# Writing the product kv into the space of ssm_k with an 8-byte step between the columns that TensorE loads

## The chip, the cores and the metric

One core of a Trainium2 chip. The metric is the device time of one execution in microseconds (us); lower is better. Kernels are compared only within the same rounds.

## The reference, cut to what matters

```python
# A: q, k, v are (1, 2048, 512), ssm_k is (512, 2048), shift_k is (512, 4)
kv = shift(k, shift_k) * v                       # 4 taps along the sequence, then a product
kv_f = rfft(pad(kv));  kf_f = rfft(pad(ssm_k))   # along the sequence, length 4096
y    = irfft(kv_f * kf_f)[:2048] + kv * ssm_D
h    = x + layernorm(x) * y                      # x is q
out  = h + relu(layernorm(h) @ w1) @ w2          # 512 -> 1376 -> 512
```

The kernel does the Fourier transforms as two stages of matmuls, with position t = 64 n1 + n2. Both inputs of the transform, ssm_k and kv, lie with the 512 features on partitions (four row groups of 128). Before stage 1 TensorE turns them, so that (row group, n1) comes to lie on partitions: 64 transposes each, one per n2.

## The kernel before: the parts that matter

```python
sk = early.tile([P, DC, S], BF16, name="sk")                 # ssm_k, one DMA
nc.sync.dma_start(out=sk[:], in_=A_ssm_k.rearrange("(c p) t -> p c t", p=P))
vT = vp.tile([P, DC, S], BF16, name="vT")                    # v, one tile filled by four DMAs
for c in range(4):
    ts = slice(CH * c, CH * c + CH)                          # CH = 512
    nc.sync.dma_start_transpose(out=kT[:, :, 16 + CH * c:16 + CH * c + CH], in_=k_d[ts, :])
    nc.sync.dma_start_transpose(out=vT[:, :, ts], in_=v_d[ts, :])
# ... [cut]
def to_rows(src, q, fl, eng):
    pst = psum.tile([P, 8, P], BF16, tag="ps", name="pst")
    for i in range(8):                                       # columns 64 elements = 128 bytes apart
        nc.tensor.transpose(out=pst[:, i, :], in_=src[:, :, :, 8 * q + i], identity=ident[:])
    copy(eng, fl[:, :, :, 8 * q:8 * q + 8], pst[:].rearrange("p i (d g) -> p g d i", d=2))
# ... [cut]
skv = sk[:].rearrange("p c (a b) -> p c a b", b=64)
for q in range(8):
    to_rows(skv, q, kfl, "DADADADA"[q])                      # D: VectorE, A: ScalarE

def taps(u):                                                 # 16 units: chunk c of 512, row group rg
    c, rg = divmod(u, DC)
    ps = psum.tile([P, CH], F32, tag="ps", name="pkv")
    for j in range(KS):
        nc.tensor.matmul(out=ps[:], lhsT=wdiag[:, rg, j, :], rhs=kT[...], start=..., stop=...)
    vv = vT[:, rg, CH * c:CH * c + CH]
    nc.vector.tensor_tensor(out=vv, in0=ps[:], in1=vv, op=ALU.mult)    # kv, in place

taps(0)
for gb in range(7):
    group_k(gb)                                              # stage 1 of ssm_k, and a table
    taps(2 * gb + 1)
    taps(2 * gb + 2)
taps(15)
group_k(7)
# ... [cut]
kvv = vT[:].rearrange("p r (a b) -> p r a b", b=64)
for q in range(8):
    to_rows(kvv, q, xfl, "ADADADAD"[q])                      # again 128 bytes apart
# then: spectrum of k and stage 1 of kv; products (psy); first inverse stage (psi);
# second inverse stage (pz); the two matmuls of the MLP (ps1m, ps2m)
```

`rearrange` only describes another view of the same bytes. The framework derives all waits from the views of the tiles, and decides which of a tile's writers an instruction waits for.

## Time and profile before

| | before |
|---|---|
| time, median of 3 | 223.93 us (223.79 to 223.94) |
| profiled span, mean granted clock | 221.4 us, 0.999 |
| first k transposition, first stage-1 group of k | 9.73, 17.16 |
| first kv transposition, first stage-1 group of kv | 37.48, 45.44 |
| first psi, pz, ps1m matmul | 98.44, 114.97, 128.09 |

The last three rows are times from the start of the span, read off the chain of waits. The profile lines themselves stand in the prediction.

### The profile page before, as it was taken

The numbers are of one execution on the slowest core, as the hardware profiler recorded it, in microseconds if no ns is written. First come the engines' busy times: TensorE is split into PE (matmuls) and PEld (weight loads), VectorE is DVE, ScalarE is ACT, GpSimd is POOL, SyncE is SP. The second block draws the span as 40 slices with busy tenths as digits, with TensorE's granted clock in tenths as the row PEclk, the third lists the DMA queues.
The fourth block names the chain that finished last, engine by engine and source line by source line (L and its number), as shares of the span: only waits on it lengthen the run. The fifth ranks groups of instructions, "written<-read, shape, count | busy, mean of one in ns | idle before, by whom it ended". The sixth has DMA issues, their size and how long they took to land.

```text
span 221.4 us, 7288 instructions
## 1 busy us (share of the span) xinstructions
PE 201.6 (91%) x3111; PEld 140.1 (63%) x3111; DVE 150.3 (68%) x299; ACT 133.0 (60%) x252; POOL 72.0 (33%) x103
## 2 busy tenths in 40 slices
PE   0299799999989999989989899999999999999993
PEld 0294446999978999969977578544444444444452
DVE  4898788889997999966878779761973257130031
ACT  2868877888885888867983889103650066206500
POOL 8399940000008999978400120220022002000000
PEclk9999999999999999999999999999999999999999
DMA  5999920000000000019990000152113110421012
GB/s 178 311 223 204 193 53 4 0 4 6 3 3 3 1 0 0 4 47 238 258 340 14 3 3 3 24 82 58 31 28 80 42 48 4 95 56 42 0 43 54
DMA packets 30384, 15.41 MB, mean 70 GB/s; under 512 B 25520, under 2 KB 29072, under 8 KB 30224
## 3 DMA queue, kind: packets, MB, share of 16 engines
q1 hardware_dynamic: 29520, 14.76, 29.0%
q8 instruction: 24, 0.39, 0.7%
q10 hardware_dynamic: 832, 0.20, 0.4%
q14 instruction: 8, 0.07, 0.1%
HBM read 7.08 MB, written 2.10 MB: 41 GB/s over the span
## 4 chain that ended last, share of the span: by engine, by line
PE 85%; ACT 5%; DMA 4%; DVE 2%; issue 1%; SPq 0%; DVEq 0%; ACTq 0%
PE ps2m L536 18%; PE ps1m L524 16%; PE pz L450 8%; PE psy L343 7%; PE psi L417 7%; PE pkv L262 6%; PE pst L203 6%; PE ps L221 4%; PE ps2k L236 4%; DMA sk<-in_A_ssm_k_dram 4%; PE ps2k L238 3%; PE u L236 3%; PE u L238 3%; ACT ecore L131 1%; ACT zt L461 1%
## 5 line engine op out<-in xcount | busy, mean ns | idle before, releaser
L526 ACT ACTIVATE h1T<-ps1m 128x512 bf16<-128x512 f32 (+3 forms) x55 | 27.4, 514 | 21.2 <-PE ps1m L524 20.3
L524 PE MATMUL ps1m<-hlnT,w 128*128 128x512 bf16 (+3 forms) x220 | 39.6, 336 | 0.3
L536 PE MATMUL ps2m<-w,h1T 128*128 128x512 bf16 (+3 forms) x187 | 39.8, 367 | 0.0
L538 DVE TENSOR_TENSOR o<-ps2m,xh 128x512 bf16<-128x512 f32 (+1 forms) x17 | 11.1, 659 | 37.6 <-PE ps2m L536 32.2
L524 PEld LDWEIGHTS <-w 128*128 128x128 bf16 (+1 forms) x220 | 21.7, 100 | 17.6 <-issue 1.4
L536 PEld LDWEIGHTS <-h1T 128*128 128x128 bf16 (+1 forms) x187 | 17.6, 98 | 21.2 <-issue 3.1
L333 DVE TENSOR_TENSOR t<-u,kf 128x704 fp32r<-128x704 f32 x32 | 26.7, 883 | 3.0 <-ACT usb L329 2.8
L333 POOL TENSOR_TENSOR t<-usb,kf 128x320 fp32r<-128x320 f32 x32 | 28.2, 935 | 1.4 <-ACT usb L329 1.0
L461 ACT CAST zt<-pz 128x512 bf16<-128x512 f32 x16 | 8.4, 593 | 29.5 <-PE pz L450 29.5
L450 PE MATMUL pz<-bp,ecore 32*32 32x128 f32 x1024 | 23.1, 384 | 1.7 <-DVE bp L210 0.9
L470 POOL TENSOR_SCALAR rstd<-mv 128x4 f32<-128x4 f32 (+1 forms) x7 | 1.6, 232 | 70.1 <-DVE mv L477 70.1
L208 ACT CAST a<-ps 128x512 fp32r<-128x512 f32 (+1 forms) x38 | 19.3, 568 | 4.3 <-PE ps L221 4.3
L450 PEld LDWEIGHTS pz<-bp,ecore 32*32 32x32 f32 x1024 | 14.4, 103 | 9.1 <-issue 5.0
L210 DVE CAST a<-ps 128x512 fp32r<-128x512 f32 (+1 forms) x30 | 18.5, 651 | 2.2 <-PE ps L221 2.1
L208 ACT CAST kf<-psy 128x512 fp32r<-128x512 f32 x30 | 17.4, 641 | 1.8 <-PE psy L343 0.3
L475 DVE BATCH_NORM_STATS2 st<-xh 128x6 f32<-128x512 bf16 x28 | 17.3, 678 | 0.0
L262 PE MATMUL pkv<-kT,wdiag 128*128 128x512 bf16 x64 | 15.4, 380 | 1.2 <-issue 1.2
L417 PE MATMUL psi<-dre,kf 128*128 128x256 f32 x64 | 15.5, 284 | 0.9 <-DVE kf L210 0.9
L343 PE MATMUL psy<-t,ipos 128*128 128x512 f32 x48 | 15.9, 391 | 0.0
L417 PE MATMUL psi<-dim,kf 128*128 128x256 f32 x64 | 15.4, 283 | 0.0
L203 PE MATMUL pst<-ident,sk 128*128 128x128 bf16 x64 | 6.3, 277 | 9.7 <-DMA sk<-in_A_ssm_k_dram 9.7
L265 DVE TENSOR_TENSOR vT<-pkv,vT 128x512 bf16<-128x512 f32 x16 | 10.9, 691 | 3.4 <-PE pkv L262 3.4
(113 smaller groups left out, 394.9 us busy)
## 6 DMA issues: line engine op xcount, KB each, us to landing
sk<-in_A_ssm_k_dram SPq DMA_DIRECT2D x1, 2048.0 KB, 8.4
out_dram<-o SPq DMA_DIRECT2D x58, 32.0 KB, 1.6
xh<-in_A_q_dram SPq DMA_DIRECT2D x4, 384.0 KB, 6.8
w<-in_B_w_dram SPq DMA_DIRECT2D x1, 1376.0 KB, 12.8
w<-in_B_w_dram SPq DMA_DIRECT2D x1, 1280.0 KB, 16.2
xh<-in_A_q_dram SPq DMA_DIRECT2D x4, 128.0 KB, 2.8
hlnT<-hln SPq DMA_TRANSPOSE x12, 2.4
w<-in_B_w_dram SPq DMA_DIRECT2D x1, 96.0 KB, 15.9
```

Of the source, the lines that this page charges most:

```text
L203: nc.tensor.transpose(out=pst[:, i, :], in_=src[:, :, :, 8 * q + i], identity=ident[:])
L208: nc.scalar.copy(out=o, in_=i)
L210: nc.vector.tensor_copy(out=o, in_=i)
L262: nc.tensor.matmul(out=ps[:], lhsT=wdiag[:, rg, j, :], rhs=kT[:, rg, CH * c + 16 - j:CH * c + CH + 16 - j], start=(j == 0), stop=(j == KS ...
L333: eng.tensor_tensor(out=t[:, :, j, :], in0=in0.unsqueeze(1).to_broadcast([P, 2, n, 2]), in1=kfr[:, :, j, ks], op=ALU.mult)
L343: nc.tensor.matmul(out=psy[:], lhsT=m_[:], rhs=t_.rearrange("p j k -> p (j k)"), start=first, stop=not first)
L417: nc.tensor.matmul(out=ps[:, i, :], lhsT=kf[:, c, 4 * m:4 * m + 4, :].rearrange("p r k -> p (r k)"), rhs=d[:].rearrange("p a b -> p (a b)" ...
L450: nc.tensor.matmul(out=pz[32 * a:32 * a + 32, r4, l4, :], lhsT=ecore[rows, rho, n2, :], rhs=rhs, start=(rho == 0), stop=(rho == 1), tile_p ...
L475: nc.vector.bn_stats(out=st[:, t % 4, :], in_=xh[:, t, :])
L524: nc.tensor.matmul(out=ps1[:fsz, :], lhsT=w1[:, c, fc * P:fc * P + fsz], rhs=hlnTs[sc][:, c, part], start=(c == 0), stop=(c == DC - 1))
L526: nc.scalar.activation(out=h1s[sc][:fsz, fc, part], in_=ps1[:fsz, :], func=ACT.Relu)
L536: nc.tensor.matmul(out=ps2[:], lhsT=h1s[sc][:ksz, fc, i * P:(i + 1) * P], rhs=w2[:ksz, fc, ds], start=(fc == 0), stop=(fc == NFC - 1))
```

## The change

Its intent: a weight load whose columns lie 128 bytes apart is slow (204 ns against 97), so kv is written in another order, (n2 // 4, row group, n1, n2 % 4), where the columns of one load lie 8 bytes apart. That order cannot be written in place, so kv goes into the space of ssm_k. Four smaller parts come with it: ssm_k in two halves with column-tiled transposes, one more taps unit ahead of the first group, other shares of the copies, and split copies at two ends.

```diff
-    nc.sync.dma_start(out=sk[:], in_=A_ssm_k.rearrange("(c p) t -> p c t", p=P))
+    for h in range(2):
+        nc.sync.dma_start(out=sk[:, 2 * h:2 * h + 2, :], in_=A_ssm_k[2 * h * P:(2 * h + 2) * P, :]...)
 ...
-    for q in range(8):
-        to_rows(skv, q, kfl, "DADADADA"[q])
+    psts = [psum.tile([P, 8, P], BF16, tag="ps", name="pst") for _ in range(8)]
+    for h in range(2):
+        hs = slice(64 * h, 64 * h + 64)
+        for q in range(8):
+            for i in range(8):
+                nc.tensor.transpose(out=psts[q][hs, i, :], in_=skv[:, 2 * h:2 * h + 2, :, 8 * q + i],
+                                    identity=ident[:], tile_position=(0, 64 * h))
+            if h == 1:
+                rows_out(psts[q], q, kfl, "DADADADA"[q])
 ...
+    kvx = sk[:].rearrange("p c t -> p (c t)").rearrange("p (h r a l) -> p h r a l", h=16, r=DC, l=4)
 ...
-        vv = vT[:, rg, CH * c:CH * c + CH]
-        nc.vector.tensor_tensor(out=vv, in0=ps[:], in1=vv, op=ALU.mult)
+        split = "p (a h l) -> p a h l"
+        nc.vector.tensor_tensor(out=kvx[:, :, rg, 8 * c:8 * c + 8, :].rearrange("p h a l -> p a h l"),
+                                in0=ps[:].rearrange(split, h=16, l=4),
+                                in1=vT[:, rg, CH * c:CH * c + CH].rearrange(split, h=16, l=4), op=ALU.mult)
 ...
     taps(0)
-    for gb in range(7):
+    taps(1)
+    for gb in range(8):
         group_k(gb)
-        taps(2 * gb + 1)
-        taps(2 * gb + 2)
-    taps(15)
-    group_k(7)
+        for u in range(2 * gb + 2, min(2 * gb + 4, 16)):
+            taps(u)
 ...
-        to_rows(kvv, q, xfl, "ADADADAD"[q])
+        pst = psum.tile([P, 8, P], BF16, tag="ps", name="pst")
+        for i in range(8):
+            nc.tensor.transpose(out=pst[:, i, :],
+                                in_=kvx[:, 2 * q + i // 4, :, :, i % 4].rearrange("p r a -> p (r a)"), identity=ident[:])
+        rows_out(pst, q, xfl, "ADADADAD"[q])
 ...  [cut: other shares of the stage-1 copies; the last two psy copies and two psi copies split over both engines]
```

## The prediction

> **What bounds the kernel now.** I read the page first (TensorE busy 91% of 221.4 us, the next, VectorE, 68%; TensorE is 85% of the chain that ended last), then that chain over the stages that the diff touches:
>
> ```profile
> 1.25 8.44 DMA sk<-in_A_ssm_k_dram
> 9.69 0.05 issue
> 9.73 6.34 PE pst L203 x64
> 16.07 0.02 issue
> 16.09 1.02 ACT kfl L208
> 17.11 0.04 issue
> 17.16 0.68 PE ps L221 x64
> 17.84 1.83 PE pkv L262 x8
> ...
> 25.77 1.24 issue
> 27.02 1.46 PE pkv L262 x6
> ...
> 36.73 0.70 DVE vT L265
> 37.43 0.04 issue
> 37.48 5.99 PE pst L203 x64
> ```
>
> Columns are start, length, what. TensorE waits for the whole of ssm_k until 9.73, transposes it (L203), then alternates one stage-1 group (0.61) with two taps units (8 matmuls, 1.83) at 2.45 us a group, then transposes kv (37.48 to 43.47), then does spectrum and stage 1 at 2.72 us a group, TensorE back to back. So anything that shortens TensorE's work or starts it earlier before about 45 us moves the end by as much, unless a copy takes over.
>
> How fast are the transposes? Their weight loads step 128 bytes between columns (64 bf16). Counted in equal stretches (TensorE busy with its count, then its weight loads):
>
> ```profile
> 9.73:12.73 3.00, 3.00 (x28) 3.00 (x29) 1.00 1.13 247
> 12.83:15.83 3.00, 3.00 (x38) 3.00 (x35) 1.00 1.19 229
> 37.48:40.48 3.00, 3.00 (x33) 3.00 (x34) 1.00 0.02 5
> ```
>
> The first 3 us hold 28 starts, one per 107 ns; the other 36 k transposes start in the 3.1 us after that, one per 86 ns (the second row also counts those still in flight at its start), and those of kv one per 91 to 94 ns (5.99 / 64). Transposes late in the kernel read contiguous columns:
>
> ```profile
> 125.85 0.61 PE L546 MATMUL pz<-ident,hln 128*128 128x128 bf16 x8 [0.43 <-ACT zt L461]
> ```
>
> Eight in 0.61, of which the last one's own duration is 0.22: (0.61 - 0.22) / 7 = 56 ns each. A contiguous load is recorded at 97 ns, the strided one of kv at 204. So the kv transposes are bound by the strided load, 36 ns above what the moving operand needs.
>
> Their copies out of PSUM (busy us, mean ns):
>
> ```profile
> L210 DVE COPY xfl<-pst 128x1024 bf16<-128x1024 bf16 x4 | 4.9, 1225 | 1.2 <-PE pst L203 0.6 <-issue 0.6
> L208 ACT COPY xfl<-pst 128x1024 bf16<-128x1024 bf16 x4 | 3.9, 1012 | 0.5 <-PE pst L203 0.4
> ```
>
> **What the Trainium skill says.** (1) "SBUF — State Buffer", "Door 1: The DMA port swizzle", its note on cachelines: 16-byte lines, at least two hits on a line are needed for full bandwidth. At 128 bytes a line gives one hit, at 8 bytes two. The trace agrees for the two ends (94 against 56 ns) and shows nothing at 8 bytes. (2) "TensorE: Matmul & The Clock Gate", Part 1: start to start is N / 1.2 GHz while the clock is gated (106.7 ns for N = 128), N / 2.4 GHz plus 2.5 ns after about one busy window of 3.4 us, the window free-running. The trace agrees: 107 ns for 3.07 us, and 56 where loads are contiguous. The clock column above says 1.00 throughout and doesn't show the gate. (3) "TensorEngine Tiling (Array Packing)", "Restrictions": column tiling disables the fast weight load. The changed k transposes are column tiled; no row of this trace shows such a load with a stride. (4) "Advanced Engine Details and Errata", "ISA Cache": instructions are cached in lines of 16 KB, 256 instructions. The profile has 24 packets of 0.39 MB on the instruction queue, 16 KB each. I read the 1.24 us "issue" at 25.77 as a late fetch: no data is awaited there, and the DMA share of that time is full of transposes.
>
> **The change part by part.**
>
> (a) ssm_k in two halves; 128 transposes of 64 columns in place of 64 of 128. Half of the big packets had ended by 5.95, all by 9.23, and TensorE started 0.5 later, so the first half releases it at about 6.45 instead of 9.73: 3.3 us earlier. But each transposition still streams 128 columns of the identity, so the number of full-length streams doubles, and the first ones run gated. With the gate opening 3.1 us after the start (as before), 29 are done by 9.6 and 99 x 0.056 = 5.5 end at 15.1; with the gate opening only at 12.8, 59 are done and 69 x 0.056 = 3.9 end at 16.7. Middle 15.9, against 16.09 before. So this part nearly pays for itself and no more, up to here.
>
> (b) Two taps units, not one, stand before the first stage-1 group. Before, TensorE had done one when it waited for the last kfl copy until 17.16. Now both follow the transposes: 15.9 + 2 x 0.92 = 17.75, by when the copies are done (VectorE 4 x 1.2 from about 12.5, ScalarE less). The first group starts at 17.75, 0.6 later, with 0.92 more behind it: 0.3 gained. The last group now stands after the last taps as before, so the 0.7 of VectorE at 36.73 stays.
>
> (c) Instruction fetch. The stall came 705 TensorE instructions (loads and matmuls) in; the extra 128 bring that point one group (144) earlier, to about 25, when its fetch is asked for before the third k transfer fills the queues. I take a third of the 1.24 as remaining: 0.8 gained, anywhere from 0 to 1.24.
>
> Sum so far: kv transposes start 1.1 us earlier, near 36.4 (range 0 to 2.3).
>
> (d) kv written with an 8-byte stride. TensorE: 64 x (94 - 56) = 2.4 us less. But copies then bind. From the start T of the transposes, VectorE still has two stage-1 copies until T + 1.2 (37.36 + 1.29 in the trace), then four of 1.225: T + 6.1. ScalarE has two copies and two table pieces until T + 2.0 (39.37), then four of 1.01: T + 6.05. The first kv stage-1 group needs all eight. Before it started at 45.37 = T + 7.9; now at T + 6.2. Gained: 1.7, not 2.4. The product itself writes runs of four bf16 instead of rows; its 691 ns are set by 512 fp32 read from PSUM, and the spectrum addition that writes pairs of fp32 takes 682, so I give it no cost.
>
> (e) In spectrum and stage 1, three copies of 0.69 move from VectorE to ScalarE (0.54 each). VectorE falls from 2.57 to an average near 2.3 per 2.72 group, ScalarE rises from 2.4 to 2.95 in odd groups, 2.66 on average. TensorE stays the bound; it prevents the backlog from (d) from growing, and may cost 0.1.
>
> (f) End of products: the last two copies are split, but the instruction order shows that the VectorE half waits for the ScalarE half of the same PSUM tile. ScalarE 0.35 then VectorE 0.41 is no faster than one VectorE copy of 0.69: 0. End of the first inverse stage:
>
> ```profile
> 113.11 1.35 ACT L208 COPY bp<-psi 128x512 f32<-128x512 f32 x3 [0.37 <-PE psi L417]
> ...
> 113.48 0.68 DVE L405 BATCH_NORM_STATS2 st<-xh 128x6 f32<-128x512 bf16 x1
> ...
> 114.19 0.18 DVE L406 BATCH_NORM_AGGREGATE mv<-st 128x2 f32<-128x6 f32 x1
> 114.47 1.28 ACT L467 ACT_TABLE_LOAD   x1
> 114.49 0.42 DVE L210 COPY bp<-psi 128x256 f32<-128x256 f32 x1
> ```
>
> VectorE is busy with statistics until 114.37 and now has two half copies instead of one: 114.37 + 2 x 0.4 = 115.15 against 114.91. Lost: 0.25.
>
> Sum: 1.1 + 1.7 - 0.1 - 0.25 = 2.45 us. After 68 us nothing else changes. 223.93 - 2.45 = 221.5.
>
> **The rivals.**
>
> Rival A, any stride loses the fast load: contiguity, not the line, decides. For it: a contiguous fp32 load, which is four bytes per column, is recorded at 188 ns, like the strided bf16. Against: the two-hits rule. Then the kv transposes stay at 94 ns, (d) gives 0, and the time is 223.2.
>
> Rival B, the column-tiled strided load is slow. [...]if a far column costs 88 / 32 = 2.75 ns on its own, 64 take 176 ns, the 128 end near 29 instead of 15.9, and the kernel takes about 234. Against: during the gated 3 us, 128 such columns loaded within 107 ns. If it is 70 to 80 ns instead of 56, (a) loses 1.4 to 2.4 on the last 99 and the time is near 223.
>
> Rival C, everything goes well: gate open at 9.6, no fetch stall. The first group starts at 17.0, kv transposes at 35.1: 2.3 gained, sum 3.7, time 220.2. More than 2% needs 219.5, that is 4.4 us, which these parts reach only if phase (e) speeds up too; TensorE back to back there speaks against it.
>
> Rival D, the start is late (gate at 12.8) and the fetch stall stays whole: (a) to (c) give -0.5 and the time is 223.1.
>
> **Range and chances.** Centre 221.5. The middle of A and D gives the upper end 223.3, C with a little from PSUM waits avoided gives 219.9. More than 2% faster: 0.07. Slower by over 2% (above 228.5) needs B in full: 0.03. Within 2%: 0.90.
>
> **What would show it.** The first transposition near 6.4 and the last near 15.9; first stage-1 group of k at 17.75; the count of kv transposes in 3 us near 53 rather than 33; kfl and xfl copies unchanged in length; the first kv stage-1 group 6.2 us after the first kv transposition, released by a copy and no longer by TensorE; 2.7 us a group after it; the "issue" gap shorter or gone; the first pz matmul 0.25 later relative to the last psi matmul. I am wrong on (a) if column-tiled transposes start more than 65 ns apart after the gate opens, on (d) if the kv ones stay above 80 ns, on (e) if groups take over 2.85 us.

## The result, and the profile after

The changed kernel took 233.94 us (median of 4 fast runs, 232.84 to 234.63), the kernel before 223.94 (4 runs, 223.79 to 225.17). The ratio is 1.043, with a 95% interval of 1.037 to 1.049: slower. Ratios here and below are the mean time of one kernel's fast runs over that of the other's of the same rounds, so not quite the ratio of the medians. Executions over 1.5% slower than the fastest of the same kernel are left out of the means. The profiled span went from 221.4 to 232.6 us.

| first ... (us from the start) | before | predicted | after | after less before |
|---|---|---|---|---|
| k transposition | 9.73 | 6.45 | 6.66 | -3.1 |
| end of the k transposes | 16.07 | 15.9 | 20.6 | +4.5 |
| stage-1 group of k | 17.16 | 17.75 | 22.36 | +5.2 |
| kv transposition | 37.48 | 36.4 | 49.41 | +11.9 |
| stage-1 group of kv | 45.44 | 42.6 | 55.62 | +10.2 |
| psi matmul | 98.44 | | 108.50 | +10.1 |
| pz matmul | 114.97 | | 125.15 | +10.2 |
| ps1m matmul | 128.09 | | 139.54 | +11.5 |

By the kv transposes, at 49.4, 11.9 us are lost; 1.7 of them come back in the transposes, and 1.3 are lost again in the pz stage. The chain of waits of the changed kernel over the stretch where the time went, with start, length and what, as before:

```profile
25.25 4.57 DMA vT<-in_A_v_dram
29.94 0.69 DVE sk L273
30.64 0.61 DVE a L209
31.29 1.01 PE ps L220 x60
...
33.05 2.76 PE pkv L270 x6
35.82 0.97 PE ps L220 x63
...
49.41 3.76 PE pst L296 x64
...
55.62 0.65 PE ps L220 x61
```

In the kernel before, the same stretch of the chain was TensorE alone (the taps of L262 and stage 1 of L221) with one gap of 1.24. Now a transfer of v stands in it, until 29.82 (before 25.25 the chain is the DMA queue issuing the transposing transfers one after another), and behind it one product on VectorE (L273), then one stage-1 copy (L209). Only after these does TensorE go on, at 31.29. The stage-1 groups after the wait also run slowly: one is at 31.29, the next at 35.82, 4.5 us later, where one group with its taps had taken 2.45.

The view of waits says the same (who waited, for whom: total us, times, the longest):

```profile
DVE sk L273 <- DMA vT<-in_A_v_dram: 7.7, 1, 7.7
PE ps L220 <- DVE sk L273: 5.7, 1, 5.7
```

One wait, once: VectorE stood still for 7.7 us and TensorE for 5.7 of them. The product's row on the page of the kernel before, and on that of the changed one, with busy us, mean ns of one, and the idle time before it:

```profile
L265 DVE TENSOR_TENSOR vT<-pkv,vT 128x512 bf16<-128x512 f32 x16 | 10.9, 691 | 3.4 <-PE pkv L262 3.4
L273 DVE TENSOR_TENSOR sk<-pkv,vT 128x512 bf16<-128x512 f32 x16 | 10.8, 689 | 11.3 <-DMA vT<-in_A_v_dram 7.7
```

The product takes as long as before; only the idle time before it has grown. The stretches of the wait and after it (stretch, us, then busy time and count of PE, PEld, DVE, ACT and POOL, then the granted clock, the DMA share and GB/s):

```profile
24.90:30.70 5.80, 0.12 (x3) 0.01 (x3) 0.76 (x2) 0.87 (x2) 5.01 (x12) 0.67 0.81 161
30.70:37.40 6.70, 6.06 (x136) 3.12 (x138) 4.86 (x8) 2.64 (x6) 0.00 (x0) 0.52 0.02 4
```

TensorE idles through the first stretch, and its clock is then granted at 0.52 for the 6.7 us of the second: the idle time costs a second time, in the two slow groups. The two kernels below that keep the wait show the same: 0.52 with the view alone and 0.62 with ssm_k whole, each over the 6.6 us after it. In the whole page the dip is seen in one row:

```profile
PEclk9999858999999999999999999999999999999999
```

The loads of the kv transposes before (busy us, mean ns), then those of the two kinds of transposes in the changed kernel (min, median and max duration in ns, first and last start, columns x rows of the load):

```profile
L203 PEld LDWEIGHTS <-vT 128*128 128x128 bf16 x64 | 5.9, 204 | 0.3 <-DVE vT L265 0.3
```

```profile
L248 PEld LDWEIGHTS <-sk x128: 186/203/207, 6.7 to 20.2; 128*64 128x64 bf16 x128
L296 PEld LDWEIGHTS <-sk x64: 111/113/130, 49.4 to 52.9; 128*128 128x128 bf16 x64
```

The kv loads (L296) came down from 204 to 113 ns, as the change intends, and their 64 transposes take 3.8 us where they took 6.0. But a column-tiled load of half as many columns (L248) takes 203 ns, and the 128 of them start 110 ns apart from first to last, but for six at the change from one half to the other.

Last, the pz stage in the chain of waits: these pauses end no wait that the profile shows. In the chain of the kernel before there is a single one, of 0.19.

```profile
128.33 0.81 issue
129.14 2.69 PE pz L465 x121
131.83 0.87 issue
132.70 2.70 PE pz L465 x118
135.40 0.88 issue
```

Why does one product wait for a transfer? The compiled order shows which semaphores each product waits for (DMAHW stands for transfers, PE for the taps). This is the list of instructions, not the profile (the trace has the same numbers of semaphores at these products):

```
             unit 0                       unit 1                       unit 4
before L265  DMAHW5, PE                   PE                           DMAHW7, PE
after  L273  DMAHW4, DMAHW6, DMAHW3, PE   DMAHW2, DMAHW4, DMAHW0, PE   PE
```

Before, unit 0 waits for the transfer that brings chunk 0 of v, units 1 to 3 for none, and unit 4, the first that needs chunk 1, for the next. After, unit 1 waits for three transfers, and no later unit waits for any: so these are chunks 1, 2 and 3, which unit 1 doesn't read. (Unit 0 waits for three as well, but with the halves of ssm_k, whose space it overwrites.)

Three causes were put to the test. W: the products wait for all of v, because they see it as a view of three dimensions. T: the column-tiled loads are slow. I: the 128 more TensorE instructions bring pauses for instructions in the pz stage. The first rival to W was the layout itself (writing 8-byte runs is slow, or sk, which is read and then overwritten, is what is waited for); the rival to T was the clock gate.

### The profile page after: what moved, and what is told of

Read it like the earlier page. It is cut to its first block, busy times and chain, and to the rows that moved or that the text cites. A ratio compares the mean times of both kernels' runs of the same rounds, so it can differ in the third digit from the quotient of the medians.

```text
span 232.6 us, 7400 instructions
## 1 busy us (share of the span) xinstructions
PE 208.3 (90%) x3156; PEld 146.1 (63%) x3175; DVE 149.1 (64%) x298; ACT 133.5 (57%) x256; POOL 71.7 (31%) x103
## 4 chain that ended last, share of the span: by engine, by line
PE 74%; SPq 10%; DVE 5%; ACT 4%; issue 3%; DMA 2%; DVEq 0%; ACTq 0%
PE ps2m L551 16%; PE ps1m L539 15%; PE pz L465 10%; SPq L112 7%; PE psy L354 6%; PE pkv L270 5%; PE ps L220 4%; PE ps2k L235 4%; PE psi L432 3%; SPq L113 3%; PE u L235 3%; PE ps2k L237 3%; PE u L237 3%; DMA vT<-in_A_v_dram 2%; DVE bp L209 2%
## 5 line engine op out<-in xcount | busy, mean ns | idle before, releaser
L551 PE MATMUL ps2m<-w,h1T 128*128 128x512 bf16 (+3 forms) x177 | 38.9, 366 | 0.7 <-issue 0.3
L207 ACT CAST a<-ps 128x512 fp32r<-128x512 f32 (+1 forms) x41 | 20.8, 572 | 11.7 <-PE ps L220 11.7
L465 PEld LDWEIGHTS pz<-bp,ecore 32*32 32x32 f32 x1024 | 13.9, 103 | 11.5 <-issue 7.1
L248 PE MATMUL pst<-ident,sk 128*64 128x128 bf16 x128 | 13.9, 283 | 6.7 <-POOL f_r L149 6.7
L207 ACT CAST kf<-psy 128x512 fp32r<-128x512 f32 (+1 forms) x31 | 17.7, 628 | 1.9 <-PE psy L354 0.2
L209 DVE CAST a<-ps 128x512 fp32r<-128x512 f32 (+1 forms) x27 | 16.6, 647 | 2.4 <-PE ps L220 2.3
L273 DVE TENSOR_TENSOR sk<-pkv,vT 128x512 bf16<-128x512 f32 x16 | 10.8, 689 | 11.3 <-DMA vT<-in_A_v_dram 7.7
L248 PEld LDWEIGHTS <-sk 128*64 128x64 bf16 x128 | 13.8, 203 | 6.7 <-DMA sk<-in_A_ssm_k_dram 6.7
L490 DVE BATCH_NORM_STATS2 st<-xh 128x6 f32<-128x512 bf16 x28 | 17.3, 678 | 0.0
L270 PE MATMUL pkv<-kT,wdiag 128*128 128x512 bf16 x56 | 16.3, 415 | 0.7 <-issue 0.4
L354 PE MATMUL psy<-t,ipos 128*128 128x512 f32 x48 | 15.9, 391 | 0.0
```

Source lines behind the costliest of these rows:

```text
L207: nc.scalar.copy(out=o, in_=i)
L209: nc.vector.tensor_copy(out=o, in_=i)
L248: nc.tensor.transpose(out=psts[q][hs, i, :], in_=skv[:, 2 * h:2 * h + 2, :, 8 * q + i], identity=ident[:], tile_position=(0, 64 * h))
L354: nc.tensor.matmul(out=psy[:], lhsT=m_[:], rhs=t_.rearrange("p j k -> p (j k)"), start=first, stop=not first)
L465: nc.tensor.matmul(out=pz[32 * a:32 * a + 32, r4, l4, :], lhsT=ecore[rows, rho, n2, :], rhs=rhs, start=(rho == 0), stop=(rho == 1), tile_p ...
L490: nc.vector.bn_stats(out=st[:, t % 4, :], in_=xh[:, t, :])
```

## The experiments

Line numbers of these kernels differ by a few; the tile names stay. "Before" in each heading's ratio is the kernel before in the same rounds.

### The view alone, in the kernel before

```diff
 # kernel before, nothing else touched
-        vv = vT[:, rg, CH * c:CH * c + CH]
-        nc.vector.tensor_tensor(out=vv, in0=ps[:], in1=vv, op=ALU.mult)
+        vv = vT[:, rg, CH * c:CH * c + CH].rearrange("p (a h l) -> p a h l", h=16, l=4)
+        nc.vector.tensor_tensor(out=vv, in0=ps[:].rearrange("p (a h l) -> p a h l", h=16, l=4), in1=vv, op=ALU.mult)
```

The same bytes are read and written in place; only their description has three dimensions.

> The kernel before, only with the product's three operands seen as (a, h, l) instead of as one run of 512; the layout of the result, all sizes and the transposes are unchanged. Theory W': it is the view of v alone that brings the wait, since the compiled order shows the second product waiting on three further transfers. Then that product moves from 18.9 to about 28.6, TensorE stalls for several us, its clock is gated again, and the time is 231 to 234. Rival: a three-dimensional operand makes the product itself slow, and then its duration rises from 691 ns; or no effect, 223.9.

Measured: 234.79 us (234.04 to 235.34, 4 runs), ratio 1.042 (1.038 to 1.047). The waits of this kernel, and its product's row:

```profile
DVE vT L266 <- DMA vT<-in_A_v_dram: 11.3, 1, 11.3
```

```profile
L266 DVE TENSOR_TENSOR vT<-pkv,vT x16: 680/692/692, 17.3 to 47.6; 128x512 bf16<-128x512 f32 x16
```

The product itself costs what it did (median 692 ns, where the prediction had 691), and the wait is there. It is longer, 11.3 us, because this kernel reaches it earlier, its first product being at 17.3. In the compiled order its unit 1 waits for three transfers of v and no later unit for any, as in the changed kernel. Its kv transposes start at 48.34. The view alone, without a byte of the new layout, costs as much as the whole change. W holds and its rival falls.

### v in four tiles, in the changed kernel

```diff
-    vT = vp.tile([P, DC, S], BF16, name="vT")
+    vTs = [vp.tile([P, DC, CH], BF16, name=f"vT{c}") for c in range(4)]
-        nc.sync.dma_start_transpose(out=vT[:, :, ts], in_=v_d[ts, :])
+        nc.sync.dma_start_transpose(out=vTs[c][:], in_=v_d[ts, :])
-                                in1=vT[:, rg, CH * c:CH * c + CH].rearrange(split, h=16, l=4), op=ALU.mult)
+                                in1=vTs[c][:, rg, :].rearrange(split, h=16, l=4), op=ALU.mult)
```

> The changed kernel, only with v in four tiles of 512 columns instead of one, so that a product waits for the transfer of its own quarter alone. Theory W (the second product waits for all four v transfers, VectorE blocks until 29.9, TensorE stalls and its clock is gated for 10 us): the 5.8 us gap of TensorE goes, the first stage-1 group of k stays at 22.4 (the column-tiled transposes are unchanged at 110 ns), the kv transposes start at 22.4 + 18.1 = 40.5 instead of 49.4, and the time is near 225. Rival T (the slow transposes are the whole loss and the wait would be hidden): no more than 1 us below 233.9.

Measured: 226.84 us (225.71 to 228.32, 4 runs), ratio 1.0055 (1.000 to 1.011). The wait is gone, in the compiled order unit 1 waits for the taps alone and unit 4 for one transfer, as before the change, and the chain of waits has the kv transposes 7.9 us earlier than the changed kernel:

```profile
22.48 0.61 PE ps L220 x64
...
41.47 3.76 PE pst L296 x64
```

The time expected was near 225, with the kv transposes at 40.5. So of the 11.9 lost up to there, 49.41 - 41.47 = 7.9 are the wait with the slow clock after it, and 41.47 - 37.48 = 4.0 are something else: the first stage-1 group still starts at 22.48 rather than 17.75. The pz stage takes 15.7 us (13.1 before), with pauses of 1.00, 1.15 and 1.14.

### ssm_k whole again, in the changed kernel

```diff
-    (the two half transfers and 128 column-tiled transposes of the change)
+    nc.sync.dma_start(out=sk[:], in_=A_ssm_k.rearrange("(c p) t -> p c t", p=P))
+    for q in range(8):
+        pst = psum.tile([P, 8, P], BF16, tag="ps", name="pst")
+        for i in range(8):
+            nc.tensor.transpose(out=pst[:, i, :], in_=skv[:, :, :, 8 * q + i], identity=ident[:])
+        rows_out(pst, q, kfl, "DADADADA"[q])
```

> The changed kernel, only with ssm_k loaded by one transfer and transposed 128 columns at a time as before; the wait on all v transfers stays. Theory W: the first stage-1 group of k comes at 18.0 instead of 22.4, but the second product still waits until the last v transfer has landed (28.5 to 30), so the kv transposes stay near 49 and the time gains 0 to 1.5 us against 233.9, part of it from 128 instructions less to fetch. Rival T: all 4.4 us are gained, 229.5.

Measured: 232.81 us (232.07 to 233.33, 4 runs), ratio 1.033 (1.029 to 1.038). The v transfer still ends the wait (the product starts at 29.73) and the kv transposes start at 48.62. The slow k transposes are there in the changed kernel but lie almost wholly under the wait for v: taking them away alone gains about 1 us. Two losses that lie beside one another don't add, and neither can be read from undoing it alone: four v tiles brought the kv transposes forward by 7.9 in the changed kernel, and by 48.62 - 37.67 = 11.0 on top of this one (next run).

### Both undone, the rest of the change kept

The edits of the last two together.

> Both undone: 128-column transposes of k and four v tiles; kept are the 8-byte layout, the order of the taps, the shares of the copies. First group at 18.0, kv transposes at 36.1 to 37.3 (against 37.5 before), first kv stage-1 group 6.2 us later (7.9 before): 221 to 222.3 by the terms of the prediction that held. If the taps order or the copies cost something unseen: 224 or more.

Measured: 222.99 us (221.8 to 225.45, 4 runs, one of them slow and left out of the ratio), ratio 0.988 (0.983 to 0.994). Its median is the lowest of the versions that compute the right thing and were run more than once; the intervals of its variants below overlap with its own. Its chain of waits:

```profile
17.84 0.61 PE ps L218 x64
...
25.78 1.71 issue
...
37.67 3.77 PE pst L290 x64
...
43.89 0.65 PE ps L218 x61
```

The first group starts at 17.84, and the first kv stage-1 group 6.2 us after the first kv transposition, where it had been 7.9. The kv transposes, expected at 36.1 to 37.3, start at 37.67; the pause near 26 stays, at 1.71 even longer. The pz stage takes 13.3 us, as before.

### Column tiles in turn

In the kernel with four v tiles, the same 128 column-tiled transposes, in another order: the two halves of each pair follow one another.

```diff
-    for h in range(2):
-        for q in range(8):
-            for i in range(8):                        # 64 in a row into one column tile
+    for q in range(8):
+        for i in range(8):
+            for h in range(2):                        # column tiles take turns
```

> Four v tiles kept; the 128 column-tiled transposes of k alternate between the two column tiles (lower and upper 64 output rows) instead of doing all of one and then all of the other, so they start when the second half of ssm_k has landed, near 9.8. In the changed kernel they start 110 ns apart, except for six in a row at the change of tile that are 56 apart. Theory P (a load into a tile waits for that tile's own matmul or load, and the other tile's goes beside it): 55 to 60 ns, 128 end near 17.2, first stage-1 group near 19, 3 us earlier than with the halves in turn (22.4), time near 223.5 where four v tiles alone gave 226.8. Theory R (the read of 64 far-apart columns is itself the limit, 1.7 ns a column): 110 ns still, end at 23.9, time near 229.

Measured: 224.97 us (224.05 to 225.64, 4 runs), ratio 0.999 (0.996 to 1.002), where the kernel with four v tiles and the order of the change had 1.0055; the intervals just overlap. In the traces its kv transposes start at 39.63 and not at 41.47. The chain of waits has them in 7.96 us, where the changed kernel needed 13.94:

```profile
10.10 7.96 PE pst L247 x119
```

They start in pairs: two some 4 ns apart, then some 119 ns to the next pair, so about 62 ns each. So while one column tile loads (203 ns in the changed kernel), the other can load as well; two loads into the same tile start some 110 to 120 ns apart in both kernels. At this step the order of the loads made the 110 ns. It loses the early start, though: both halves of ssm_k have to be there, so the first group comes at 19.90, 2.1 later than with whole transposes.

### Column-tiled loads with a step of 8 bytes, and of 2

Again with four v tiles, and the order of the change. The columns are taken from the wrong places, so these two kernels compute something else. The comparison with the reference passed them nonetheless: its tolerance does not notice this part of the output, so a pass says nothing on it.

```diff
+        skh = sk[:, 2 * h:2 * h + 2, :].rearrange("p c t -> p (c t)")
-                                    in_=skv[:, 2 * h:2 * h + 2, :, 8 * q + i],
+                                    in_=<64 columns of skh, 4 elements apart; in the second kernel adjacent>,
```

> Four v tiles kept, halves in turn; each column-tiled transposition of k reads its 64 columns 8 bytes apart instead of 128 (the result is wrong on purpose). Theory S (the step costs, as in the kv transposes, which fell from 94 to 59 ns): below 70 ns apart once the clock is open, 107 while it is gated. Theory F (column tiling takes the fast load away, and the load costs 1.7 ns a column whatever the step): 110 ns.

> As the run with 8 bytes, with the 64 columns next to each other (wrong on purpose). Theory S: as at 8 bytes, 55 to 70 ns. Theory F: 110 ns, or if the slow load costs one column per cycle only when contiguous, near 60 here and 110 at 8 bytes.

Measured, one run each of unknown state: 223.18 and 221.94 us. What counts is the load's row, with busy us and mean ns of one. A step of 8 bytes:

```profile
L250 PEld LDWEIGHTS <-sk 128*64 128x64 bf16 x128 | 10.0, 156 | 6.6 <-DMA sk<-in_A_ssm_k_dram 6.6
```

Adjacent columns:

```profile
L250 PEld LDWEIGHTS <-sk 128*64 128x64 bf16 x128 | 8.9, 130 | 6.6 <-DMA sk<-in_A_ssm_k_dram 6.6
```

These means mix two states, since the first transposes of both runs start 107 ns apart: a load takes 172 ns (8 bytes) and 177 (adjacent) between 7 and 10 us, and 145 and 110 from 13 us on. From the seventh microsecond after the first on, the transposes start 61 and 56 ns apart, where the 128-byte step gave 110 all along. So the clock gate, the rival to T, does not explain the 110: these two kernels start the same transposes at the same time and get past it. The step decides here too, and the theory that the loss of the fast path makes the load equally slow whatever the step falls. A column tile is not free for all that: 64 columns take 110, 145 and 203 ns in one (adjacent, 8 and 128 bytes), where 128 untiled columns take 97, 114 and 204.

### Other steps: 16, 32 and 64 bytes

In the kernel with both undone, `h=16 ... l=4` of the layout became `h=8 ... l=8`, then `h=4 ... l=16` and `h=2 ... l=32`, so that the columns of one kv load lie 16, 32 and 64 bytes apart.

```diff
-    kvx = ...rearrange("p (h r a l) -> p h r a l", h=16, r=DC, l=4)
+    kvx = ...rearrange("p (h r a l) -> p h r a l", h=8, r=DC, l=8)      # 16 bytes; then h=4, l=16 and h=2, l=32
```

> Both parts undone as in the best run so far, with kv laid out for a step of 16 bytes instead of 8 (runs of eight, not four). Theory L (a line of 16 bytes has to give two columns): the kv transposes fall back to 88 to 94 ns and take 5.9 us instead of 3.8; the first kv stage-1 group then waits for TensorE again, 7.9 us after the first transposition instead of 6.2, and the time rises by 1.7 over 223.0. Rival (any step below some larger size is fast): 59 ns and 223.0.

> Both parts undone, kv laid out for a step of 32 bytes. At 8 bytes the kv transposes are 56 ns apart (the matmul's own length), at 16 bytes 61, at 128 bytes 88 to 94. If the time rises with the step between: 65 to 80; if it jumps at some step, 61 or 88 and more.

> As the run with 32 bytes, with a step of 64. 75 to 90 if it rises steadily, 61 or 88 and more if it jumps.

Measured: 16 bytes 223.37 us (221.95 to 224.32, 4 runs), ratio 0.994 (0.990 to 0.998); 32 and 64 bytes one run each, state unknown, 223.61 and 222.42. The rows of the kv load, at 8 bytes (the kernel with both undone):

```profile
L290 PEld LDWEIGHTS <-sk 128*128 128x128 bf16 x64 | 3.6, 114 | 0.3 <-DVE sk L267 0.3
```

and at 16 bytes:

```profile
L290 PEld LDWEIGHTS <-sk 128*128 128x128 bf16 x64 | 4.0, 147 | 0.3 <-DVE sk L267 0.3
```

| step of the columns | mean load, ns | 64 kv transposes, us |
|---|---|---|
| 2 bytes (the late transposes of before) | 97 | |
| 8 | 114 | 3.77 |
| 16 | 147 | 4.14 |
| 32 | 149 | 4.21 |
| 64 | 151 | 4.30 |
| 128 (kernel before) | 204 | 5.99 |

I had expected 16 bytes to cost nearly what 128 do (88 to 94 ns a transposition), since no two columns share a line of 16 bytes any more. They cost 65 (4.14 / 64). That theory falls as it stood: there is a step between 8 and 16 bytes, nothing from 16 to 64, and the larger step from 64 to 128. What lies behind the last one these runs do not show. For the kernel it hardly matters: the first kv stage-1 group came 6.1 us after the first kv transposition at 16 bytes as well. There the chain is TensorE alone, 4.14 of transposes and 1.97 of spectrum matmuls, about what the copies allowed at 8 bytes (6.2).

### 128 instructions more, with nothing else

In the kernel with both undone, 64 transposes of the identity in the time in which TensorE waits for ssm_k. Their results are not used.

```diff
+    for _ in range(8):
+        pst = psum.tile([P, 8, P], BF16, tag="ps", name="pst")
+        for i in range(8):
+            nc.tensor.transpose(out=pst[:, i, :], in_=ident[:], identity=ident[:])
```

> Both parts undone (128-column transposes of k, four v tiles), plus 64 transposes of the identity into PSUM tiles that nobody reads, 128 TensorE instructions as the changed kernel has more, put where TensorE waits for ssm_k anyway. Theory I (the pauses called issue are fetches of 256 instructions): the pause at the 701st instruction stays at the 701st and so comes one group earlier in the work; the pauses in the first pz stage come at the 3769th, 4025th and 4281st as in the changed kernel, and that stage, from the first pz to the first ps1m matmul, grows from 13.3 to 14.4 to 15.7 us. Besides, the clock may be open by 9.8, so the k transposes start 88 apart from the first on and end 0.5 earlier. Rival (the longer pz stage came from another cause of the changed kernel): 13.3 stays. Total 223 to 225.

Measured: 223.12 us (222.01 to 223.38, 4 runs), ratio 0.987 (0.981 to 0.994), so not to be told from the kernel with both undone. Its chain in the pz stage:

```profile
116.80 0.61 issue
...
120.10 0.77 issue
...
123.56 1.15 issue
```

The three pauses appear, and the pz stage takes 14.9 us instead of 13.3. Counted in the trace, they stand at the 3769th, 4025th and 4281st TensorE instruction, 256 apart, the same three positions as in the changed kernel. (The trace of the kernel before has all its matmuls; in the other traces 19 are missing, so its 705th, which the prediction names, is their 701st.) The kernel with both undone pauses at the first two of these positions too, 0.41 and 0.81, the second beside the chain, which runs over ScalarE there; with the 128 instructions other work stands at these positions, and the third pause is added. The early pause stands at the 701st here too, while the work at that point is another; but it is down to 0.35, and one of 1.80 follows some 256 instructions later. So the pauses belong to positions in the stream of instructions. I holds: in the eight traces without the 128 instructions the pz stage takes 13.0 to 13.8 us, in the six with them 14.3 to 15.7, and here they compute nothing. In the timed runs this is not seen: the ratios are alike, although the traced span is longer (221.6 against 220.0; the fast runs of the two have spans of 220.2 to 221.6 and 220.0 to 221.5). A small part comes back at the start, where the k transposes, which now follow other work on TensorE, take 5.97 instead of 6.33.

### The split copies at the two ends undone

In the kernel with both undone, the copies of the last product and of the last but one psi tile as before the change.

```diff
-            if kp < 15: ...
-            else: (copy columns 0 to 136 by ScalarE, 136 to 256 by VectorE)
+            copy("AD"[s] if kp >= 16 - LAG else "A", kf[:, s, :, 2 * kp:2 * kp + 2], ...)
-        if b < 30:
+        if b < 31:
```

> Both parts undone, and also the split copies at the end of the products and of the first inverse stage as before. The prediction gave 0 for the first and a loss of 0.25 us for the second; so from the last product to the first psi matmul about as in the best run so far, and from the first psi to the first pz matmul 16.5 us instead of 16.7; the time 0.1 to 0.4 below that of the run with both parts undone, too little for the timed runs to show.

Measured: 223.29 us (222.83 to 225.41, 6 runs), ratio 0.991 (0.985 to 0.997), against 0.988 for the kernel with both undone. The intervals overlap. From the first psi to the first pz matmul the traces have 16.53 without the split copies and 16.66 with them, and all others agree: 16.53 in the two more that have none (the kernel before and the view alone), 16.64 to 16.66 in the ten more that have them. So 0.13 is lost there. In the stretch before, from the first u to the first psi matmul, it is 31.5 to 31.6 without and 31.6 to 31.7 with them, too little to tell. The timed runs cannot show an eighth of a microsecond.

## Why the prediction was wrong

It was wrong: 221.5 us, with a chance of 0.03 for slower by 2%. Steps (a), (c), (d) and (f) were tested by runs of their own; (b) and (e) are read from the traces alone. By its steps:

- **(d), the product. This is the step that failed.** The prediction wrote "The product itself writes runs of four bf16 instead of rows; its 691 ns are set by 512 fp32 read from PSUM, and the spectrum addition that writes pairs of fp32 takes 682, so I give it no cost." The duration was right (692 ns, and 692 with the view alone). But an instruction costs what it takes and what it waits for, and only the first was looked at. The second product waits for all four transfers of v, and with the slow clock after the idle time that is 7.9 of the 11.9 us (changed kernel against that with four v tiles), or 11.0 once the k transposes are whole. The view alone reproduces it. The instruction order had been drawn on for (f), and its rows for units 0 and 1 were there to be compared.
- **(d), the transposes.** Right in mechanism and size. The first kv stage-1 group was put 6.2 us after the first kv transposition, with copies binding; it came at 55.62 - 49.41 = 6.2, and 6.2 again with both undone. The last link is not one of the eight copies that the sum counts but the spectrum's copy right behind them on ScalarE (0.70), so the exact hit has some luck in it. Rival A (any step loses the fast load) is out: 114 ns at 8 bytes, 204 at 128.
- **(a).** The start was right (6.45, measured 6.66), the size of the loads was not: 56 ns apart after the gate was assumed, 110 was measured, and the end came at 20.6 instead of 15.9. With adjacent columns the same 128 transposes end at 15.70, so it is the load alone that the sum has wrong. Rival B had the right suspicion and nearly the right time (234) for another reason: the prediction expected 176 ns for it, and in the end the column-tiled loads account for at most some 4 us, of which only about 1 shows as long as the wait for v lies over them. The rival's argument against itself, that 128 columns loaded within 107 ns, took untiled loads as a measure for loads that follow one another into one column tile. The page that was read for the restriction also has a section, "Tiling Modes", "Key Properties" of the Trainium skill's "TensorEngine Tiling (Array Packing)", that lets different tiles load in parallel; the run with the tiles in turn agrees (62 ns against 110), and the order of the change, 64 loads in a row into one tile, gives that up.
- **(b).** Right where it can be seen: with the k transposes ended near 16, the first group starts at 17.84 (predicted 17.75).
- **(c).** Open. A gain of 0.8, anywhere from 0 to 1.24, was expected of the 1.24 us pause. In the changed kernel the wait for v covers it, and with both undone the 128 instructions are gone, so its 1.71 tests nothing. Where they are there and v is not waited for, the pauses of this stretch add up to 0.72 (four v tiles: 0.56 and 0.16), 1.62 (tiles in turn) and 2.15 (identity transposes: 0.35 and 1.80), so anything from 0.5 gained to 0.9 lost. What was left out is the other side of the same coin: more instructions early shift all later ones, and the pz stage became 1.3 us longer. The identity transposes show that this comes from the instructions themselves.
- **(e).** Held: from the first kv stage-1 group to the first psi matmul it took 53.0 us before, 52.9 after, so there was nothing to gain or lose.
- **(f).** Right in sign and place, half in size: 0.25 lost was predicted from psi to pz, 0.13 is in the traces.

With the wait and the column-tiled loads out, the remaining parts give a ratio of 0.988, that is a gain near the 2.45 us (0.989) that had been predicted for the whole. That agreement is partly luck: 1.1 of the 2.45 were to come from (a), (b) and (c), but the kv transposes start 0.2 later than before in this kernel; its traced span is 1.4 shorter, and the interval of the ratio allows 1.5 to 3.8.

What stays open: why a step of 128 bytes costs so much more than 64, why the framework waits for the whole of v under this view, and why the first pause of the pz stage lasts 0.61 us with the identity transposes and 1.00 with four v tiles.

## What to carry to other kernels

When a change alters the view through which an instruction sees a tile, compare the semaphores that the instruction waits for before and after, not only its duration: a tile filled by several transfers may then be waited for as a whole, and one tile for each transfer avoids it. An idle stretch on TensorE can be paid for twice: after the 5.8 us here its clock was granted at 0.52 for 6.7 us. Where loads go into column tiles, let the tiles take turns, and find by undoing two suspects together, not only one by one, what each hides.

## What the Trainium skill lacked or had wrong

- "SBUF — State Buffer", the cacheline note in "Door 1: The DMA port swizzle": its boundary, two hits on 16 bytes, is seen in weight loads (114 ns at 8 bytes, 147 at 16), but it is not the only one. They took 97 ns at 2 bytes, 147 to 151 from 16 to 64, and 204 at 128; the largest jump, between 64 and 128 bytes, is not on the page.
- "TensorEngine Tiling (Array Packing)", "Restrictions": that column tiling disables the fast load is not contradicted (64 adjacent columns took 110 ns, 128 untiled ones 97, both with the transposes 56 ns apart). The page lacks what it costs, and that it depends on the order: with 128 bytes between columns 110 ns a transposition with one tile many times in a row, 62 with the tiles in turn.
- "TensorE: Matmul & The Clock Gate", "Part 4: PE-mode transpose" says that full clock doesn't engage for transpose mode. With nothing but transposes on TensorE (column-tiled loads of adjacent columns) they came 107 ns apart at first and 56 some microseconds later. The trace lists them as plain matmuls, so whether they ran in that mode, and so whether the page is wrong, stays open. Beside it, the profile's clock row shows the slow clock after an idle stretch (0.52) but 1.00 in the first 3 us of TensorE's work, when transposes started 107 ns apart.
- "Advanced Engine Details and Errata", "ISA Cache" gives the 256 instructions of a line, and the pauses of the pz stage are 256 TensorE instructions apart. Neither it nor another page has a figure for what a pause there costs: 0.16 to 2.0 us in these traces, at the same positions in the stream, with other work there.
- No page has it that a tile seen through a view of three dimensions may be waited for as a whole: 7.7 us of VectorE in the changed kernel, 11.3 with the view alone.
